# Loading the first query heads' output weights on five DMA engines instead of six, with half a head as half rows on all partitions

## Chip, cores, metric

One Trainium2 chip, one core. The metric is the device time of one execution in microseconds; lower is better. Verdicts use a 2% threshold, and the chip's "fast" state.

## The reference

One decode step: adaLN modulation, grouped-query attention over a cache, a small FFN. Cut to what matters:

```python
# x [1,1,512]; k_cache, v_cache [1,8,32768,128] bf16 (64 MB each); wq [512,4096]; wo [4096,512]
mod = (silu(c) @ w_mod).reshape(...)                   # six rows of 512
h = layernorm(x) * (1 + ca) + sa
q = h @ wq                                             # 32 query heads, 4 to each of 8 kv heads
o = softmax(q k^T / sqrt(128)) v
x = x + ga * (o @ wo)                                  # wo: 128 rows of 512 for each head
h = layernorm(x) * (1 + cb) + sb
x = x + gb * (relu(h @ w1) @ w2)
```

About 149 MB are read once for very little arithmetic, so the kernel is a stream of loads with a tail.

## The kernel before

The parts that matter: `wo` is loaded in five pieces. Piece 0, the first three heads, is called the low part below (`wo_lo` in the code). It lies on 48 of 64 partitions and comes in eight transfers of six partitions, 8 KB each, between the K and V tiles of two groups. Piece 1 is one head as one row on each of 128 partitions, and so on.

```python
WOP = [(0, 3, 48), (3, 1, P), (4, 4, P), (8, 16, P), (24, 8, P)]   # first head, heads, partitions
LO = [(0, 0, 16, 0), (1, 0, 8, 16), (1, 8, 16, 32), (2, 0, 16, 40)]
...
if kind == "wo_lo":
    b, i = key[1] // 4, key[1] % 4
    stream_dma(wo_lo[32 * b + i:32 * b + i + 21:4], wo_v(0)[24 * b + i:24 * b + i + 21:4])
...
elif kind == "wo_mid":                                  # pieces 1, 2, 3 in one buffer of the ring
    t = ring.tile([P, sum(wo_rows(i) for i in key[1:]), D], BF16, tag="slot", name="wo_sb")
    for i in key[1:]: ... stream_dma(loaded[("wo", i)], wo_v(i))
...
stream += [("v", LAST, (0, 1)), ("wo_mid", 1, 2, 3), ("v", LAST, (2,)), ("v", LAST, (3,)), ("wo", 4)]
stream += [("w1",)] + [("w2", i) for i in range(len(W2P))]
```

All loads are issued by SP into one queue, q1 of the profile. The profile has two more queues of the kind "instruction", q8 with packets of 16 KB and q14 with packets of 8 KB; they are called fetches below. The attention output is spread to the layout of each piece by masks (DVE) and one small matmul (`normalise`, `spread`), and multiplied with it (`project`).

## Time and profile before

| | kernel before |
|---|---|
| three first runs | 358.30, 357.19, 358.43 us |
| span of the traced run | 356.4 us |
| 16 DMA engines busy with the stream (q1) | 97.7% of the span |
| last packet of the stream | 352.20 us |
| from that packet to the end | 4.2 us |

The first thing to read is the share of q1 and the row of DMA digits, the second which DMA engine ends last. The profile has no view of single DMA engines. But the trace has start, duration and size of each packet, and an engine works without a pause, so a packet that starts where another one ended belongs to the same engine. This gives sixteen chains. Where two chains are in step to a few nanoseconds they can be mistaken for each other; the chains named below are kept apart by the packets that only they have. The prediction shows the lines; one more, on the transfers of piece 0, from the list of DMA issues (KB each):

```profile
wo_lo<-in_A_wo_dram SPq DMA_DIRECT2D x8, 48.0 KB
```

Eight issues of 48 KB, that is, 8 KB to each of six engines.

### The profile page before, as it was taken

The numbers are of one execution on the slowest core, as the hardware profiler recorded it, in microseconds if no ns is written. First come the engines' busy times: TensorE is split into PE (matmuls) and PEld (weight loads), VectorE is DVE, ScalarE is ACT, GpSimd is POOL, SyncE is SP. The second block draws the span as 40 slices with busy tenths as digits, with TensorE's granted clock in tenths as the row PEclk, the third lists the DMA queues.
The fourth block names the chain that finished last, engine by engine and source line by source line (L and its number), as shares of the span: only waits on it lengthen the run. The fifth ranks groups of instructions, "written<-read, shape, count | busy, mean of one in ns | idle before, by whom it ended". The sixth has DMA issues, their size and how long they took to land.

```text
span 356.4 us, 3625 instructions
## 1 busy us (share of the span) xinstructions
PE 287.4 (81%) x1554; PEld 127.7 (36%) x1554; DVE 194.1 (54%) x231; ACT 34.0 (10%) x78; POOL 12.0 (3%) x16
## 2 busy tenths in 40 slices
PE   0096766999779987999796969897987969899964
PEld 0053222334434443334242333333333323334563
DVE  5822967983397439372918256564718383742011
ACT  1012201301200120002000120012000100001200
POOL 9400000000000000000000000000000000000000
PEclk9999689899969998999896998999799979999855
DMA  8999999999999999999999999999999999999992
GB/s 326 436 427 443 423 449 424 423 451 425 423 436 434 421 451 434 425 436 423 440 434 423 452 426 416 452 428 414 449 430 427 440 427 445 434 411 419 428 414 83
DMA packets 6842, 149.66 MB, mean 420 GB/s; under 512 B 761, under 2 KB 890, under 8 KB 1914
## 3 DMA queue, kind: packets, MB, share of 16 engines
q1 hardware_dynamic: 6818, 149.43, 97.7%
q8 instruction: 12, 0.20, 0.2%
q14 instruction: 4, 0.03, 0.0%
q10 hardware_dynamic: 8, 0.00, 0.0%
HBM read 149.42 MB, written 0.00 MB: 419 GB/s over the span
## 4 chain that ended last, share of the span: by engine, by line
DMA 49%; PE 25%; DVE 19%; issue 5%; ACT 1%; POOL 0%; DVEq 0%; POOLq 0%
DMA Ksb<-in_A_k_cache_dram 42%; DVE KTt L413 14%; PE S_ps L422 11%; PE o_ps L496 8%; DMA Vsb<-in_A_v_cache_dram 5%; DMA w_sb<-in_B_w_dram 2%; DVE sel L184 2%; PE modT_ps L315 1%; PE mod_ps L298 1%; PE q_ps L298 1%; PE qT_ps L372 1%; PE acc_ps L486 1%; ACT L274 0%; DVE PT_g L465 0%; PE acc_ps L506 0%
## 5 line engine op out<-in xcount | busy, mean ns | idle before, releaser
L422 PE MATMUL S_ps<-KTt,qbd 128*128 128x512 bf16 x512 | 136.6, 425 | 34.4 <-DVE KTt L413 34.4
L413 DVE STREAM_TRANSPOSE KTt<-Ksb 128x2048 f32<-128x2048 f32 x64 | 142.6, 2280 | 29.3 <-DMA Ksb<-in_A_k_cache_dram 26.2
L496 PE MATMUL o_ps<-Vsb,PT_g 128*16 128x512 bf16 x480 | 108.4, 379 | 0.0
L422 PEld LDWEIGHTS <-qbd 128*128 128x128 bf16 x512 | 53.5, 105 | 111.2 <-issue 61.0
L496 PEld LDWEIGHTS <-PT_g 128*16 128x16 bf16 x480 | 40.8, 90 | 60.0 <-issue 5.9
L428 DVE TENSOR_SCALAR_CACHE_REDUCE S_g<-S_ps 128x512 f32<-128x512 f32 x16 | 11.1, 691 | 39.4 <-PE S_ps L422 39.4
L393 ACT COPY qbd<-qrep_sb 32x128 bf16<-32x128 bf16 x32 | 9.4, 295 | 160.6 <-PE S_ps L422 159.5
L465 DVE STREAM_TRANSPOSE PT_g<-P_g 128x1024 bf16<-128x1024 bf16 x8 | 9.9, 1238 | 21.7 <-ACT P_g L460 21.7
L514 DVE TENSOR_TENSOR oT_sb<-acc_ps,Linv 128x4 bf16<-128x4 f32 x8 | 1.3, 161 | 25.7 <-PE acc_ps L486 17.2
L234 PE MATMUL xc_ps<-one,c_bd 8*128 8x1 bf16 x4 | 0.3, 172 | 16.0 <-DVE rowsum L218 16.0
L506 PE MATMUL acc_ps<-osel,X 16*128 16x4 f32 x64 | 8.4, 250 | 2.5 <-ACT X L504 2.5
L457 ACT ACTIVATE nbias<-Mb_ps 128x1 f32<-128x1 f32 x8 | 1.4, 172 | 88.1 <-PE Mb_ps L455 88.1
L184 DVE COPY sel<-ident_bf 128x128 bf16<-128x128 bf16 x4 | 7.9, 3870 | 2.8 <-POOL ident_bf masks.py:199 2.8
L460 ACT ACTIVATE P_g<-S_g,nbias 128x1024 bf16<-128x1024 f32 x8 | 9.2, 1148 | 0.4 <-ACT nbias L457 0.2
L506 PEld LDWEIGHTS acc_ps<-osel,X 16*128 16x128 f32 x64 | 7.7, 186 | 3.7 <-ACT X L504 3.7
L444 DVE TENSOR_REDUCE Mrow<-mT_ps 1x4 f32<-1x128 f32 x8 | 2.2, 279 | 8.7 <-PE mT_ps L442 8.7
L504 ACT COPY X<-o_ps 16x512 f32<-16x512 f32 x8 | 4.6, 575 | 22.7 <-PE o_ps L496 22.7
L234 PEld LDWEIGHTS <-c_bd 8*128 8x128 bf16 x4 | 0.2, 114 | 16.0 <-DVE c_bd L224 16.0
L298 PE MATMUL q_ps<-wq_sb,hT 128*1 128x512 bf16 x32 | 3.6, 627 | 2.5 <-DVE hT L281 2.5
L473 DVE RECIPROCAL Linv<-L_ps 128x4 f32<-128x4 f32 x8 | 1.4, 176 | 7.0 <-PE L_ps L471 7.0
L486 PE MATMUL acc_ps<-PT_g,Vsb 128*128 128x4 bf16 x128 | 3.7, 166 | 1.6 <-DMA Vsb<-in_A_v_cache_dram 1.6
L455 PEld LDWEIGHTS Mb_ps<-ident_f,Mexp 1*128 1x128 f32 x16 | 2.3, 182 | 6.1 <-issue 6.1
(118 smaller groups left out, 102.3 us busy)
## 6 DMA issues: line engine op xcount, KB each, us to landing
Ksb<-in_A_k_cache_dram SPq DMA_DIRECT2D x16, 4096.0 KB, 29.1
Vsb<-in_A_v_cache_dram SPq DMA_DIRECT2D x15, 4096.0 KB, 23.5
wq_sb<-in_A_wq_dram SPq DMA_DIRECT2D x1, 4096.0 KB
Vsb<-in_A_v_cache_dram SPq DMA_DIRECT2D x2, 2048.0 KB, 22.7
wm_sb<-in_w_mod_dram SPq DMA_DIRECT2D x1, 3072.0 KB, 10.7
wo_sb<-in_A_wo_dram SPq DMA_DIRECT2D x1, 2048.0 KB
w_sb<-in_B_w_dram SPq DMA_DIRECT2D x1, 1792.0 KB
wo_sb<-in_A_wo_dram SPq DMA_DIRECT2D x1, 1024.0 KB, 11.1
```

The costliest lines, as they stand in the source:

```text
L184: nc.vector.tensor_copy(out=sel[:, hp, :].rearrange("p (a c) -> p a c", a=4), in_=src)
L298: nc.tensor.matmul(dst[j // 4][32 * (j % 4):32 * (j % 4) + 1, :], lhsT=src_T[:, kt:kt + 1], rhs=w[:, kt, j * 512:(j + 1) * 512], start=(kt ...
L393: nc.scalar.copy(out=o, in_=i)
L413: nc.vector.transpose(out=KTt[:].bitcast(F32), in_=Ksb[:, 32 * half:32 * half + 32, :].rearrange("p j d -> p (j d)").bitcast(F32),)
L422: nc.tensor.matmul(S_ps, lhsT=qbd[g % 2][:, hp, s, :], rhs=KTv[:, 16 * sl:16 * sl + 16, h, :, par], start=(t4 == 0 and sl == 0 and hp == 0 ...
L428: nc.vector.tensor_scalar(out=S_tiles[g][:, G, :], in0=S_ps, scalar1=1.0, scalar2=None, op0=ALU.mult, op1=ALU.max, accum_out=m_tiles[g][:, ...
L460: nc.scalar.activation(out=P_g[:], in_=S_g[:].rearrange("p g f -> p (g f)"), func=ACT.Exp, bias=nbias[:], scale=scale, accum_out=l_g[:],)
L465: nc.vector.transpose(out=PT_g[:], in_=P_g[:])
L486: nc.tensor.matmul(oT_ps, lhsT=Vsb[:, j, :], rhs=PT_g[:, j % 16, c0:c0 + REP], start=False, stop=(u == NTILE - 1 and j == TK - 1), skip_gr ...
L496: m = nc.tensor.matmul(o_tiles[g][:], lhsT=PT_g[:, j, REP * s0:REP * (s0 + 4)], rhs=Vsb.rearrange("p (s j) d -> p s j d", j=16)[:, :, j, : ...
L504: nc.scalar.copy(out=X[:], in_=o_tiles.pop(g)[:])
L506: nc.tensor.matmul(oT_ps, lhsT=X[:, s * Dh:(s + 1) * Dh], rhs=osel[:, s, :], start=(s == 0), stop=(g < LAST and s == 3), skip_group_check= ...
```

## The change

Its intent is to take the low part off one DMA engine: five partitions a transfer instead of six, and the 64 KB this leaves over (half of head 2) as 512 B half rows on all partitions, in the middle piece. `WOP` now counts rows: first row, rows on each partition, partitions. (The diff is shortened; `...` marks cuts.)

```diff
-    WOP = [(0, 3, 48), (3, 1, P), (4, 4, P), (8, 16, P), (24, 8, P)]
-    LO = [(0, 0, 16, 0), (1, 0, 8, 16), (1, 8, 16, 32), (2, 0, 16, 40)]
+    WOP = [(0, 8, 40), (320, 0.5, P), (3 * P, 1, P), (4 * P, 4, P), (8 * P, 16, P), (24 * P, 8, P)]
+    LO = [(0, 0, 16, 0), (1, 0, 4, 16), (1, 4, 16, 32), (2, 0, 8, 44)]
     def wo_v(i):
+        if i == 1:
+            return rows.rearrange("r (c d) -> (r c) d", c=2)
-            stream_dma(wo_lo[32 * b + i:32 * b + i + 21:4], wo_v(0)[24 * b + i:24 * b + i + 21:4])
+            stream_dma(wo_lo[32 * b + i:32 * b + i + 17:4], wo_v(0)[20 * b + i:20 * b + i + 17:4])
-    ... ("wo_mid", 1, 2, 3) ... ("wo", 4)
+    ... ("wo_mid", 1, 2, 3, 4) ... ("wo", 5)
-    for n in sorted({wo_rows(i) for i in range(len(WOP))}):
+    for n in (1, 2, 4, 8, 16):                              # one mask pair more
     # normalise, group 0: one large mask more; spread(1) multiplies by the row's parity
+            nc.vector.tensor_tensor(out=oA[1][:], in0=oT_sb[:, 2:3]..., in1=cmask[1][:, 64:P]..., op=ALU.mult)
+            nc.vector.tensor_tensor(out=o2[:], in0=o2_ps[:].to_broadcast([P, 2]), in1=parity[:], op=ALU.mult)
     # project(1): two matmuls of 256 columns, one for each half of a row
+                for c in range(2):
+                    nc.tensor.matmul(a_rows[0][32 * c:32 * c + 1, c * D // 2:(c + 1) * D // 2], ...)
```

More of the change, by code (lines that the diff above doesn't have):

```diff
@@ L1 @@
 from contextlib import ExitStack
+import math
 import concourse.bass as bass
@@ L68, in wo_v @@
     def wo_v(i):
-        h0, n, pp = WOP[i]
-        return A_wo[h0 * Dh:(h0 + n) * Dh, :].rearrange("(p r) d -> p r d", p=pp)
-    def wo_rows(i):
-        return WOP[i][1] * Dh // WOP[i][2]
+        r0, n, pp = WOP[i]
+        rows = A_wo[r0:r0 + int(n * pp), :]
+        if i == 1:
+            return rows.rearrange("r (c d) -> (r c) d", c=2)
+        return rows.rearrange("(p r) d -> p r d", p=pp)
     w1_v = B_w1.rearrange("(p kt) f -> p kt f", p=P)
@@ L116, in load @@
         elif kind == "wo":
-            t = ring.tile([P, wo_rows(key[1]), D], BF16, tag="slot", name="wo_sb")
+            t = ring.tile([P, WOP[key[1]][1], D], BF16, tag="slot", name="wo_sb")
             src = wo_v(key[1])
         elif kind == "wo_mid":
-            t = ring.tile([P, sum(wo_rows(i) for i in key[1:]), D], BF16, tag="slot", name="wo_sb")
+            t = ring.tile([P, sum(math.ceil(WOP[i][1]) for i in key[1:]), D], BF16, tag="slot", name="wo_sb")
             r0 = 0
             for i in key[1:]:
-                loaded[("wo", i)] = t[:, r0:r0 + wo_rows(i), :]
-                r0 += wo_rows(i)
+                n = math.ceil(WOP[i][1])
+                loaded[("wo", i)] = t[:, r0, 0:D // 2] if i == 1 else t[:, r0:r0 + n, :]
+                r0 += n
                 stream_dma(loaded[("wo", i)], wo_v(i))
@@ L151 @@
                     stream.append(("wo_lo", 4 * (g - 1) + 2 * G + (kind == "v")))
-    stream += [("v", LAST, (0, 1)), ("wo_mid", 1, 2, 3), ("v", LAST, (2,)), ("v", LAST, (3,)), ("wo", 4)]
+    stream += [("v", LAST, (0, 1)), ("wo_mid", 1, 2, 3, 4), ("v", LAST, (2,)), ("v", LAST, (3,)), ("wo", 5)]
     stream += [("w1",)] + [("w2", i) for i in range(len(W2P))]
@@ L163 @@
     wm_sb = need(("wm",))
-    wo_lo = const.tile([64, wo_rows(0), D], BF16)
+    wo_lo = const.tile([64, 8, D], BF16)
     nc.gpsimd.memset(wo_lo[:], 0.0)
@@ L205 @@
         nc.vector.tensor_copy(out=rsel[n][:], in_=rsel_f[:])
+        if n == 2:
+            parity = rsel_f
     osel = const.tile([16, 4, REP], F32)
@@ L209 @@
     oT_sb = const.tile([P, Hq], BF16)
-    oA = [const.tile([P, n, P // wo_rows(i)], BF16, name=f"oA{i}") for i, (_, n, _) in enumerate(WOP)]
-    oA[0] = const.tile([P, 1, 64], BF16, name="oA_lo")
+    oA = [const.tile([P, 64], BF16, name="oA0"), const.tile([P, 64, 2], BF16, name="oA1")]
+    oA += [const.tile([P, n, P // n], BF16, name=f"oA{i}") for i, (_, n, _) in enumerate(WOP) if i > 1]
     nc.gpsimd.memset(oA[0][:], 0.0)
@@ L514, in normalise @@
         nc.vector.tensor_tensor(out=o_g, in0=oT_ps, in1=Linv_tiles.pop(g)[:], op=ALU.mult)
-        for i, (h0, n, _) in enumerate(WOP):
+        if g == 0:
+            for h, ca, cb, p0 in LO:
+                nc.vector.tensor_tensor(
+                    out=oA[0][:, p0:p0 + cb - ca], in0=oT_sb[:, h:h + 1].to_broadcast([P, cb - ca]),
+                    in1=cmask[8][:, ca:cb], op=ALU.mult,
+                )
+            nc.vector.tensor_tensor(
+                out=oA[1][:], in0=oT_sb[:, 2:3].unsqueeze(2).to_broadcast([P, 64, 2]),
+                in1=cmask[1][:, 64:P].unsqueeze(2).to_broadcast([P, 64, 2]), op=ALU.mult,
+            )
+            spread(0)
+            spread(1)
+        for i in range(2, len(WOP)):
+            r0, n, _ = WOP[i]
+            h0 = r0 // Dh
             ha, hb = max(h0, REP * g), min(h0 + n, REP * (g + 1))
@@ L518, in normalise @@
                 continue
-            RH = wo_rows(i)
-            if i == 0:
-                for h, ca, cb, p0 in LO:
-                    nc.vector.tensor_tensor(
-                        out=oA[0][:, 0, p0:p0 + cb - ca], in0=oT_sb[:, h:h + 1].to_broadcast([P, cb - ca]),
-                        in1=cmask[RH][:, ca:cb], op=ALU.mult,
-                    )
-            else:
-                shape = [P, hb - ha, Dh // RH]
-                nc.vector.tensor_tensor(
-                    out=oA[i][:, ha - h0:hb - h0, :], in0=oT_sb[:, ha:hb].unsqueeze(2).to_broadcast(shape),
-                    in1=cmask[RH][:].unsqueeze(1).to_broadcast(shape), op=ALU.mult,
-                )
+            shape = [P, hb - ha, Dh // n]
+            nc.vector.tensor_tensor(
+                out=oA[i][:, ha - h0:hb - h0, :], in0=oT_sb[:, ha:hb].unsqueeze(2).to_broadcast(shape),
+                in1=cmask[n][:].unsqueeze(1).to_broadcast(shape), op=ALU.mult,
+            )
             if hb == h0 + n:
@@ L537, in spread @@
     def spread(i):
-        pp, RH = WOP[i][2] if i else 64, wo_rows(i)
-        o2_ps = small_ps([pp, RH], "o2_ps")
-        nc.tensor.matmul(
-            o2_ps[:], lhsT=oA[i][:].rearrange("p h c -> p (h c)"), rhs=rsel[RH][:], start=True, stop=True,
-        )
-        o2 = const.tile([pp, RH], BF16, name=f"o2_sb{i}")
-        nc.vector.tensor_copy(out=o2[:], in_=o2_ps[:])
+        pp, n = (64, 8) if i == 0 else (P, math.ceil(WOP[i][1]))
+        o2_ps = small_ps([pp, n], "o2_ps")
+        lhsT = oA[i][:] if i == 0 else oA[i][:].rearrange("p a b -> p (a b)")
+        nc.tensor.matmul(o2_ps[:], lhsT=lhsT, rhs=rsel[n][:], start=True, stop=True)
+        if i == 1:
+            o2 = const.tile([P, 2], BF16, name="o2_sb1")
+            nc.vector.tensor_tensor(out=o2[:], in0=o2_ps[:].to_broadcast([P, 2]), in1=parity[:], op=ALU.mult)
+        else:
+            o2 = const.tile([pp, n], BF16, name=f"o2_sb{i}")
+            nc.vector.tensor_copy(out=o2[:], in_=o2_ps[:])
         o2_tiles[i] = o2
     def project(i):
-        n = wo_rows(i)
+        n = WOP[i][1]
         wo_sb = need(("wo", i))
@@ L554, in project @@
                 a_rows.append(row_bank("a_ps"))
+            if i == 1:
+                for c in range(2):
+                    nc.tensor.matmul(
+                        a_rows[0][32 * c:32 * c + 1, c * D // 2:(c + 1) * D // 2], lhsT=o2_tiles[1][:, c:c + 1],
+                        rhs=wo_sb, start=False, stop=False, skip_group_check=True,
+                    )
+                return
             for r in range(n):
```

## The prediction

> **What bounds the kernel now.** I read the page first: the row of slices, the queues and the chain that ended last.
>
> ```profile
> span 356.4 us, 3625 instructions
> ...
> DMA  8999999999999999999999999999999999999992
> ...
> q1 hardware_dynamic: 6818, 149.43, 97.7%
> q8 instruction: 12, 0.20, 0.2%
> q14 instruction: 4, 0.03, 0.0%
> ```
>
> From the second slice to the 39th the sixteen DMA engines are busy 90% or more, and queue q1 alone fills 97.7% of their time: the kernel is a stream of 149 MB. The next question is whether some stage of the stream waits for buffers. I set the issue times of the loads against the start of their first packets in the trace. A 4 MB load moves in about 9.7 us, and from the start to the last V tiles each load is issued 6.6 to 26 us before its first packet; the shortest leads are 6.65 us (the first K half of group 2) and 7.25 us (the last V step). After that the lead shrinks to 3.4 us (last piece of wo), 3.1 (w1), 2.95, 2.06 and 1.18 (the three pieces of w2), but the queue still isn't empty. So PE, DVE and SP are beside the stream until its last load lands, and only the stream's length and the tail behind it set the end. The chain of waits, in order of time, has that tail:
>
> ```profile
> 323.98 17.39 DMA Vsb<-in_A_v_cache_dram
> ...
> 341.41 1.88 PE acc_ps L486 x64
> 343.30 0.02 issue
> 343.31 8.59 DMA w_sb<-in_B_w_dram
> 351.90 0.04 issue
> 351.94 0.60 PE ffn_ps L645 x16
> 352.54 0.04 issue
> 352.58 0.41 PE ffn_ps L645 x8
> 352.99 0.02 issue
> 353.01 0.30 DVE o_rows L651
> ```
>
> The last matmuls start at 352.58 because the last piece of w2 has just landed. What follows (8 matmuls, two DVE operations, the store) takes 356.4 - 352.2 = 4.2 us and isn't touched.
>
> A load has landed when its slowest DMA engine is through. The trace has start, duration and size of every packet, and an engine's packets lie back to back, so they can be linked into sixteen chains. All 4,096 packets of 32 KB have a median of 1,213 ns: no engine is slower per packet. But the chains don't end together. The six that carry the eight 8 KB packets of the low part of wo end their last w2 packet at 352.20, 351.21, 350.57, 349.95, 349.6 and 349.5 us; of the ten others one ends at 350.27 and the rest between 347.5 and 349.4. One engine is 1 us behind the next and about 3.5 us behind the middle of the field. It began its stream early; what put it back is the eight 8 KB packets, 312 ns each from period to period (9,993 ns from one to the next, against 9,681 for a plain 4 MB load), hence 2.50 us, and two instruction fetches of queue q8, at 33 and 314 us. Each took a gap of 0.87 us plus a packet of 1,764 instead of 1,213 ns: 1.42 us. The second-last engine has the same wo load and two fetches of 8 KB (q14), 0.83 and 0.84 us.
>
> **What the Trainium skill says.** "DMA: Bandwidth & Descriptors", section "Why a DMA increments its semaphore by 16 and not by 1": a transfer issued by SP runs on the largest number k of engines, at most 16, that divides the slowest dimension of both sides, and on the lowest-numbered k. Six partitions then mean engines 0 to 5, five mean 0 to 4. The trace agrees for six: the 48 packets of 8 KB fall in eight groups of six, always on the same six chains. Five no run here shows yet. "Runtime: NRT & Kernel Launch", section "Instruction fetch mechanics": instructions come in blocks of 16 KiB, over a DMA queue of the sequencer's own. The trace agrees: the twelve packets of q8 have 16,384 B. The DMA page's "Bandwidth" section, on small descriptors, gives a fixed overhead per packet, so half rows of 512 B should cost little more than their bytes; I size them from the trace below.
>
> **The change part by part.**
>
> *Low part of wo.* Eight transfers of 6 x 8 KB become eight of 5 x 8 KB. Engines 0 to 4 keep 8 x 312 ns = 2.50 us each; engine 5 loses all of it.
>
> *Half rows.* The 64 KB set free come as 128 runs of 512 B, eight an engine. A packet of 1 KB took 46 ns and one of 2 KB 84, which is 37 ns per KB over some 8 ns fixed: 27 ns for 512 B (an estimate). Starts of consecutive 1 KB packets lie 42 ns apart, four less than their duration, so 8 x 23 plus some 9 for the semaphore packet = 0.19 us on every engine.
>
> *Sum per engine.* Engine 5: -2.50 + 0.19 = -2.31 us. All others: +0.19 us. Bytes are the same.
>
> *Issue.* The eight small issues stay (0.70 us each on SP); one of about 0.35 us is added ahead of the middle piece of wo. It goes out at 306.7 for packets that start at 319.9, 13 us of lead: hidden.
>
> *Front.* A row count of 2 is new, so DVE builds one more mask pair: 0.19 + 0.28 + 0.07 = about 0.54 us on the front's DVE chain at 13 to 15 us. The loads that wait for the front have 16 to 17 us of lead, those of the following groups at least 6.6: hidden.
>
> *Normalise of group 0.* At 96.5 us DVE makes four small masks, one large (0.28 us) and two casts. One LO row shortens, one large multiply (0.3 us) is added, a 128x2 multiply takes the place of one cast (the head's own spread keeps another), and PE gets one more 0.2 us spread. Together at most 0.7 us, at a place where the stream's lead is over 9 us: hidden.
>
> *Projection.* Two matmuls of 256 columns join 21 of 512 that take about 1.8 us at 332 to 335 us. At most 0.2 us later, w1's buffer comes free; w1 had 3.1 us of lead, and PE later stands idle 1.7 us for the last V step. Hidden.
>
> So all that counts is which engine ends last. If engine 5 is the one that now ends at 352.20, it falls to about 349.9, and the next, 351.21 + 0.19 = 351.40, becomes the last: -0.80 us at the end of the stream. The landing of the last V step is set by the same two chains (341.0 and 340.0 us), so attention's tail moves by the same amount and doesn't eat it. If engine 5 is one of the other five, the last engine only gets the half rows: +0.19 us.
>
> **Rivals.**
>
> 1. *Engine 5 isn't the last.* The trace numbers no engine. For it being the last: fetches of q8 go round eight engines (the ninth hits the same as the first), of which this one alone is among the six, one is 6 or 7, and six carry neither c's eight small packets nor wo's, so they are 8 to 15; a fetching set that reaches high is likelier to include 5 than 0 to 4. Engine 0 can be excluded, since its chain has the single 1 KB packet of x. Against it: that is all. And a change so fiddly is made by someone who has seen that sixth engine lag. I give it 75%. Otherwise +0.2 us.
>
> 2. *A fetch takes the place of the saving.* The fetches fall where the instruction count puts them; a dozen more instructions could move one of 1.4 us onto another loaded engine, or into the last 20 us. The second-last engine would then be the last at about 352.4. The order round the engines speaks against it. It would make the change worth nothing to +0.5 us.
>
> 3. *A wait replaces a transfer.* The extra transfer shifts the completion semaphores by one, so a late load could wait for an earlier one. The lead of the w2 pieces is 1.2 to 3 us, and loads eight before them have landed by then. Worth at most a few tenths; unlikely.
>
> 4. *The average counts, not the last engine* (bytes are the same, so nothing changes, 0.0). Against it: the tail's wait ends within 0.4 us of the slowest chain's last packet.
>
> **Range and chances.** The stated 358.3 is the median of 357.19, 358.30 and 358.43; such a median may come out some tenths lower when repeated, so I take 358.2. With 75% at -0.80, 25% at about +0.2: 358.2 - 0.6 + 0.05 = 357.6 us. The runs before spread by 1.2 us, more than the effect, so the range is 356.7 to 358.6. Two per cent would be 7.2 us; nothing that the change touches is that large (the whole low part of wo costs 2.5 us on an engine). Within 2%: 97%; faster 2%, slower 1%.
>
> **What would show it.** In the changed kernel's trace: 40 packets of 8 KB from the low part, on five chains; 128 packets of 512 B near 320 us, about 27 ns each; the chain with two fetches of q8 without 8 KB packets of wo's low part and ending near 350 us; the last packet of w2 near 351.4 instead of 352.2, on the chain with the two 8 KB fetches; DMA digits unchanged; front and normalise later by half a microsecond without idle time in the stream. The prediction is wrong if the twice-fetching chain still has the 8 KB packets (then +0.2), if gaps other than fetches appear in the chains, or if the tail behind the last packet is longer than 4.2 us.

## The result, and the profile after

357.42 us, median of 357.28, 357.36, 357.48 and 357.55, against 357.78 for the kernel before, median of 357.19, 357.26, 358.30 and 358.43. Ratio 0.9989, 95% interval 0.9966 to 1.0012: the same at 2%, and the interval includes 1. A later series gave 0.9986 (0.9966 to 1.0006).

The page of the changed kernel, same lines as before:

```profile
span 355.4 us, 3638 instructions
...
DMA  8999999999999999999999999999999999999993
...
q1 hardware_dynamic: 6946, 149.43, 98.0%
q8 instruction: 12, 0.20, 0.2%
q14 instruction: 4, 0.03, 0.0%
```

Still a full stream with the same bytes, 1.0 us shorter; q1 has 128 packets more, the half rows. Its DMA issues of `wo`'s early pieces (KB each; the 17.4 is us from issue to landing):

```profile
wo_lo<-in_A_wo_dram SPq DMA_DIRECT2D x8, 40.0 KB
wo_sb<-in_A_wo_dram SPq DMA_DIRECT2D x1, 128.0 KB, 17.4
wo_sb<-in_A_wo_dram SPq DMA_DIRECT2D x1, 64.0 KB
```

The chain of waits at the end (start us, length us, what):

```profile
323.91 16.54 DMA Vsb<-in_A_v_cache_dram
340.45 0.05 issue
340.50 1.88 PE acc_ps L491 x64
342.38 0.02 issue
342.39 8.62 DMA w_sb<-in_B_w_dram
...
351.69 0.41 PE ffn_ps L667 x8
352.10 0.02 issue
352.12 0.30 DVE o_rows L673
```

The last V tile is used at 340.50 instead of 341.41, the last eight matmuls start at 351.69 instead of 352.58, and everything behind keeps its length. In the packets: 40 of 8 KB in the low part's time on five chains, 128 of 512 B at 27 ns, and the last packet of w2 at 351.34 instead of 352.20. It is now on the chain that had two 8 KB fetches. The chain that is gone from the low part is the one with the two 16 KB fetches (at 33.0 and 314.0 us), so that chain is engine 5. (No trace numbers the engines; here and below the numbers follow from the rule that the prediction cites.)

The added work beside the stream, DVE in the normalisation of group 0 (start us, busy us, engine, line, operation, operands, count), before and then after:

```profile
96.22 0.16 DVE L514 TENSOR_TENSOR oT_sb<-acc_ps,Linv 128x4 bf16<-128x4 f32 x1 [1.22 <-PE acc_ps L506]
...
97.19 0.35 DVE L545 CAST o_sb<-o_ps 64x8 bf16<-64x8 f32 x2
97.45 2.30 DVE L413 STREAM_TRANSPOSE KTt<-Ksb 128x2048 f32<-128x2048 f32 x1
```

```profile
96.51 0.16 DVE L519 TENSOR_TENSOR oT_sb<-acc_ps,Linv 128x4 bf16<-128x4 f32 x1 [1.22 <-PE acc_ps L511]
...
97.30 0.28 DVE L539 TENSOR_TENSOR oA<-oT_sb,cmask 128x128 bf16<-128x128 bf16 x1
97.51 0.15 DVE L560 CAST o_sb<-o_ps 64x8 bf16<-64x8 f32 x1
97.66 0.16 DVE L557 TENSOR_TENSOR o_sb<-o_ps,rsel_f 128x2 bf16<-128x2 f32 x1
97.91 0.16 DVE L560 CAST o_sb<-o_ps 128x1 bf16<-128x1 f32 x1
97.99 2.30 DVE L418 STREAM_TRANSPOSE KTt<-Ksb 128x2048 f32<-128x2048 f32 x1
```

From the first operation to the next transpose it takes 1.48 instead of 1.23 us, and it starts 0.3 us later. None of it reaches the end, where the same tail comes 0.9 us earlier.

So the pair of traces shows what was predicted, and a bit more of it: -0.86 us at the last packet. But the four runs of each kernel don't. The changed kernel's lie within 0.3 us; those of before are two near 357.2 and two near 358.4, and the traced one (358.14) is of the slower kind. A steady saving of 0.8 would have made the four into two groups near 356.4 and 357.6. This was the open question for the experiments.

### The profile page after: what moved, and what is told of

Read it like the earlier page. It is cut to its first block, busy times and chain, and to the rows that moved or that the text cites. A ratio compares the mean times of both kernels' runs of the same rounds, so it can differ in the third digit from the quotient of the medians. Undisturbed runs are those within 1.5% of the kernel's fastest.

```text
span 355.4 us, 3638 instructions
## 1 busy us (share of the span) xinstructions
PE 287.3 (81%) x1557; PEld 128.0 (36%) x1557; DVE 194.9 (55%) x236; ACT 34.0 (10%) x78; POOL 12.0 (3%) x16
## 4 chain that ended last, share of the span: by engine, by line
DMA 49%; PE 25%; DVE 19%; issue 5%; ACT 1%; POOL 0%; DVEq 0%; POOLq 0%
DMA Ksb<-in_A_k_cache_dram 42%; DVE KTt L418 14%; PE S_ps L427 11%; PE o_ps L501 8%; DMA Vsb<-in_A_v_cache_dram 5%; DMA w_sb<-in_B_w_dram 2%; DVE sel L186 2%; PE modT_ps L320 1%; PE mod_ps L303 1%; PE q_ps L303 1%; PE qT_ps L377 1%; PE acc_ps L491 1%; ACT L279 0%; DVE rsel_f L203 0%; DVE PT_g L470 0%
## 5 line engine op out<-in xcount | busy, mean ns | idle before, releaser
L303 PE MATMUL mod_ps<-wm_sb,siluT 128*1 128x512 bf16 x24 | 3.6, 624 | 1.1 <-DVE siluT L297 1.1
```

Source lines behind the costliest of these rows:

```text
L303: nc.tensor.matmul(dst[j // 4][32 * (j % 4):32 * (j % 4) + 1, :], lhsT=src_T[:, kt:kt + 1], rhs=w[:, kt, j * 512:(j + 1) * 512], start=(kt ...
```

## The experiments

Theory: the end is set by the DMA engine that ends last, whatever the mean does. Rivals: the mean load counts; the added or removed work of PE and DVE counts; and, for the two groups, something in the start or the tail differs instead of the stream.

**The kernel before against itself** (no edit).

> The kernel before, unchanged, against itself. Its four runs so far lie in two groups, 357.2 and 358.4 us. Theory (the engine that ends last): the groups differ in what delays the last engine; in a trace of a 358.4 run (span about 356.4) the last packet of w2 comes at 352.2 on the chain with two 16 KB fetches and the low wo packets; in a trace of a 357.2 run (span about 355.3) that chain ends about 1 us earlier and the one with two 8 KB fetches (351.2) is the last. Rival (the tail or the start differs, not the stream): a 357.2 run has the same last packet near 352.2 and a shorter tail than 4.2 us. Ratio 1.000, within 0.002.

Measured: 357.13 to 358.61 us (median 358.38, ratio 1.001). Of the 11 reference runs in this series five lie between 357.10 and 357.42 and six between 358.32 and 358.56; nothing between. The traced run took 358.61, with the last packet at 352.57:

```profile
342.51 9.77 DMA w_sb<-in_B_w_dram
352.28 0.04 issue
352.32 0.60 PE ffn_ps L645 x16
```

Here the 16 KB fetches hit engine 5 not at 33 and 314 us but at 109 and 345. The delay shows in the low packets: the chain that starts a low packet at 107.49 starts the next at 118.91, 1.42 us later than the 9.99 of the other groups. Hence the new theory on the groups. The fetches visit eight engines in a fixed order, but the place at which the round begins differs from run to run. The packets that they stretch show it: in the first trace these take 1,764, 1,762, 1,707, 1,712, 1,719, 1,681, 1,672 and 1,694 ns, and here the same row comes, to some 10 ns, two places earlier (1,681, 1,694, 1,764, 1,764, 1,707, ...). Twelve fetches over eight engines means two for four of them. Engine 5 gets two or one, and one fetch is 1.42 us.

**Five engines, the half head left out** (half a head is missing. Its output is wrong, which doesn't matter for the time. The comparison still called it correct, so it doesn't notice half a head).

```diff
-                stream_dma(loaded[("wo", i)], wo_v(i))
+                if i != 1:
+                    stream_dma(loaded[("wo", i)], wo_v(i))
...
             if i == 1:
+                return
                 for c in range(2):
```

> The changed kernel without the half rows (transfer and two matmuls taken out; wrong result on purpose). Theory: all chains end 0.19 us earlier than in the changed kernel, the last packet of w2 near 351.15 instead of 351.34, time about 357.2. Rival (the mean load of the engines sets the end): 64 KB less is 0.04% of the bytes, 0.15 us less; cannot be told from the theory here, but the half rows' price is read from it. Rival (the added DVE and PE work costs): nothing changes, since spread and masks are kept.

Measured: 357.20 us (357.09 to 357.54), last packet 351.28, against 351.34 for the changed kernel (0.06 earlier, expected 0.19) and 357.42. The chains of one engine begin up to half a microsecond apart from run to run, so single traces can't size 0.19. The transfer itself can be read in the changed kernel: its eight packets begin at 321.388 and the first 1 KB packet behind them at 321.582, 0.194 us.

**Six engines, and the half rows besides.**

```diff
-            t = ring.tile([P, sum(wo_rows(i) for i in key[1:]), D], BF16, tag="slot", name="wo_sb")
-            r0 = 0
+            t = ring.tile([P, 1 + sum(wo_rows(i) for i in key[1:]), D], BF16, tag="slot", name="wo_sb")
+            r0 = 1
+            stream_dma(t[:, 0, 0:D // 2], A_wo[0:64, :].rearrange("r (c d) -> (r c) d", c=2))
```

> The kernel before, and the half rows loaded besides (64 KB more, not used). Theory: every chain +0.19 us, so the last packet at the kernel before's plus 0.19, and none of the saving: slower than the changed kernel by 0.2 to 1.2 us, according to which group of the kernel before it falls into. Rival (the gain came from the half rows' smaller transfers or from the fourth piece of the middle load): as fast as the changed kernel.

Measured: 357.16, 357.25, 357.43, 357.47 and 358.50, 358.58: both groups, as the kernel before, so the half rows didn't bring the gain. The traced run, 357.47, is of the fast group, and it is the trace that tells most about it. Its end (chain of waits):

```profile
351.81 0.04 issue
351.85 0.41 PE ffn_ps L646 x7
352.26 0.02 issue
```

Engine 5 is hit by a 16 KB fetch once in it, at 242 us, and ends at 351.26, though it has all its low packets and the half rows; the chain with two 8 KB fetches ends at 351.50 and is last. In the two slow traces so far engine 5 was hit twice.

**Four engines**: heads 0 and 1 in the low part, heads 2 and 3 as two rows on all partitions.

```diff
-    WOP = [(0, 3, 48), (3, 1, P), (4, 4, P), (8, 16, P), (24, 8, P)]
-    LO = [(0, 0, 16, 0), (1, 0, 8, 16), (1, 8, 16, 32), (2, 0, 16, 40)]
+    WOP = [(0, 2, 32), (2, 2, P), (4, 4, P), (8, 16, P), (24, 8, P)]
+    LO = [(0, 0, 16, 0), (1, 0, 16, 32)]
-            stream_dma(wo_lo[32 * b + i:32 * b + i + 21:4], wo_v(0)[24 * b + i:24 * b + i + 21:4])
+            stream_dma(wo_lo[32 * b + i:32 * b + i + 13:4], wo_v(0)[16 * b + i:16 * b + i + 13:4])
```

> Two heads on four engines (8 transfers of 4 x 8 KB), heads 2 and 3 as two rows on all partitions: engine 4 gives up its low packets too, all engines get 0.3 us more than in the kernel before (eight 2 KB packets for eight 1 KB ones). Theory with the twice-8-KB-fetched chain being engine 4: that chain ends near 349.0 and the next, about 350.4 to 350.6, becomes last: 0.7 us faster than the changed kernel, about 356.7. If it is one of engines 0 to 3: last packet near 351.45, 357.5, no gain. The 16 KB fetches say engine 5; the order says nothing of engine 4: even chances. Rival (mean load sets the end): same as the changed kernel.

Measured: 357.40 us (357.32 to 357.61), last packet 351.41, on the chain with two 8 KB fetches, which still has low packets. So that engine isn't 4, and taking the load off another one of the six brought nothing. The mean rival says the same here; the next two runs part them.

**Two more looks at the kernel before.**

> The kernel before again, one look. New theory, of the two groups of its times: the 16 KB fetches go round eight engines, always in the same order, but start at another place in each execution; there are twelve of them, so four engines get two and four get one. If engine 5 gets two (two of the four places of the start seen so far), it ends last, near 352.2 to 352.6, and the run takes 358.2 to 358.6 us. If it gets one, the chain with two 8 KB fetches is last, near 351.2, and the run takes 357.1 to 357.5. Either way time and number of fetches on engine 5 go together. Rival (the start of the stream varies): they don't.

> As before_look_2: one more look at the kernel before, to have a trace of its other group. Two fetches on engine 5: 358.2 to 358.6 us and the last packet near 352.4; one: 357.1 to 357.5 and near 351.2.

Measured: 358.35 and 358.34 us, last packets 352.42 and 352.41, engine 5 hit twice in both (the first, at 33 us, shows in the low packets: its first one comes at 88.77, those of four other chains at 87.1 to 87.5). All nine reference runs of this series, on another chip than the last, were of the slow group too: 358.22 to 358.63.

**Three engines**, after the pattern of the change.

```diff
-    WOP = [(0, 8, 40), (320, 0.5, P), (3 * P, 1, P), (4 * P, 4, P), ...]
-    LO = [(0, 0, 16, 0), (1, 0, 4, 16), (1, 4, 16, 32), (2, 0, 8, 44)]
+    WOP = [(0, 8, 24), (192, 0.5, P), (2 * P, 2, P), (4 * P, 4, P), ...]
+    LO = [(0, 0, 12, 0), (0, 12, 16, 32), (1, 0, 8, 36)]
-            stream_dma(wo_lo[32 * b + i:32 * b + i + 17:4], wo_v(0)[20 * b + i:20 * b + i + 17:4])
+            stream_dma(wo_lo[32 * b + i:32 * b + i + 9:4], wo_v(0)[12 * b + i:12 * b + i + 9:4])
-                out=oA[1][:], in0=oT_sb[:, 2:3]...
+                out=oA[1][:], in0=oT_sb[:, 1:2]...
```

> One and a half heads on three engines (8 transfers of 3 x 8 KB), the other half head as half rows, heads 2 and 3 as two rows on all partitions. In the run with four engines the twice-8-KB-fetched chain kept its low packets and ended last at 351.41, so it is one of engines 0 to 3. Theory, if it is engine 3: it loses 2.5 us, and the last is one with two 16 KB fetches at 350.3 to 350.6 plus 0.5, about 350.9: 0.4 to 0.5 us faster than the changed kernel. If it is 0 to 2: last packet near 351.6, 0.2 us slower than the changed kernel. Rival (mean load): same as the changed kernel.

Measured: 356.64 us (356.42 to 356.99), ratio to the kernel before 0.9951 (0.9938 to 0.9963), last packet 351.04. The low packets are now on three chains, none of which had an 8 KB fetch before them, so the chain with two 8 KB fetches is engine 3. The last chain is now one with two 16 KB fetches, as expected, at 77 and 336 us. The traced run, 356.99, is the slowest of the five. The end of its chain of waits:

```profile
342.21 8.52 DMA w_sb<-in_B_w_dram
350.73 0.04 issue
350.77 1.00 PE ffn_ps L667 x22
```

**Two engines**: one head in the low part, heads 1 to 3 in pieces of one and two rows on all partitions.

```diff
-    WOP = [(0, 3, 48), (3, 1, P), (4, 4, P), ...]
-    LO = [(0, 0, 16, 0), (1, 0, 8, 16), (1, 8, 16, 32), (2, 0, 16, 40)]
+    WOP = [(0, 1, 16), (1, 1, P), (2, 2, P), (4, 4, P), ...]
+    LO = [(0, 0, 8, 0), (0, 8, 16, 32)]
-            stream_dma(wo_lo[32 * b + i:32 * b + i + 21:4], wo_v(0)[24 * b + i:24 * b + i + 21:4])
+            stream_dma(wo_lo[32 * b + i:32 * b + i + 5:4], wo_v(0)[8 * b + i:8 * b + i + 5:4])
-    ... ("wo_mid", 1, 2, 3) ... ("wo", 4)
+    ... ("wo_mid", 1, 2, 3, 4) ... ("wo", 5)
```

> One head on two engines (8 transfers of 2 x 8 KB), heads 1 to 3 in pieces of one and two rows on all partitions (0.64 us more on every engine than in the kernel before). Theory, if the twice-8-KB-fetched chain is engine 2 or 3: it ends near 349.4, the last is a chain with two 16 KB fetches at about 350.9 to 351.2: 0.2 to 0.4 us faster than the changed kernel. If it is 0 or 1: last packet near 351.85, 0.4 us slower than the changed kernel. Rival (mean load): same as the changed kernel.

Measured: 356.64 us (356.54 to 356.74), ratio 0.9951 (0.9937 to 0.9965), last packet 350.77. The engine hit by fetches at 32.8 and 312.6 us, engine 5 by its place in the round, is in this trace too; without low packets it ends at 350.53, not last. The chain with two 8 KB fetches, engine 3, ends at 349.33 (expected 349.4), and the last has two 16 KB fetches at 77 and 336 us. The end of the chain of waits:

```profile
344.16 6.95 DMA w_sb<-in_B_w_dram
351.11 0.04 issue
351.15 0.41 PE ffn_ps L645 x8
```

The mean load is the same in all these kernels but for packet overhead, which *grows* from six engines to two. The time falls all the same: the mean doesn't set the end.

**The changed kernel again, and looks at the kernel before.**

> The changed kernel again. Theory (the start of the fetches' round differs from run to run, and engine 5 no longer can be last): one group of times, 357.2 to 357.6, wherever the round starts; the last packet near 351.3 to 351.4 on engine 3, the chain with two 8 KB fetches. Ratio to the kernel before 0.997 if all of its runs are of the slow group (358.2 to 358.6), 1.000 if all are of the other (357.1 to 357.5). Rival (the change shortened something else by a fixed amount): the ratio is the same whatever group the kernel before is in.

> The kernel before, one look, hoped to fall into the fast group. As before_look_2: with one 16 KB fetch on engine 5, 357.1 to 357.5 us and the last packet near 351.2 to 351.5 on engine 3; with two, 358.2 to 358.6 and near 352.4 on engine 5.

> One more look at the kernel before, for the same reason. With one 16 KB fetch on engine 5, 357.1 to 357.5 us and the last packet near 351.2 to 351.5 on engine 3; with two, 358.2 to 358.6 and near 352.4 on engine 5.

> The kernel before a last time, for a trace of its fast group; the run with six engines and half rows (357.47 us, one 16 KB fetch on engine 5, last packet 351.50) stands in for it so far. With one 16 KB fetch on engine 5: 357.0 to 357.5 us and the last packet near 351.2 to 351.5, on engine 3; with two: 358.1 to 358.6 and near 352.1 to 352.6, on engine 5. The theory falls if a run of about 357.2 shows two fetches on engine 5, or one of about 358.4 only one.

Measured: the changed kernel 357.11 to 357.23 us in six runs, one group, last packet 351.30. In the same series the kernel before had six runs of 358.06 to 358.44 (mean 358.28) and five of 356.84 to 357.12 (mean 356.98). Against the mean of the changed kernel, 357.17, that is -1.11 us and +0.19 us (in the first series, split in the same way, -0.95 and +0.19). Looks 4 and 5 took 358.22 and 358.06 us, last packets 352.30 and 352.13; look 6 was traced at 358.40, 352.47, and one of its other runs took 357.09. All three have two fetches on engine 5. So of seven traces of the kernel before, seven are slow and have two; a fast one was never caught in a trace. For the fast group stand only the six-engine run with half rows, the +0.19 us, and a sum: in the seven slow traces the chain with two 8 KB fetches is second-last and ends 0.98 to 1.25 us before engine 5. With one fetch (1.42 us) less on engine 5 that chain would be last, and the run that much shorter, which is an estimate from these traces; the two groups lie 1.14 to 1.30 us apart in the four series that have both.

| traced run | 16 KB fetches on engine 5 | low packets on it | last packet, us | time, us |
|---|---|---|---|---|
| before, seven traces | 2 | 8 | 352.13 to 352.57 | 358.06 to 358.61 |
| six engines and half rows | 1 | 8 | 351.50 (another engine) | 357.47 |
| changed, first trace | 2 | 0 | 351.34 (another engine) | 357.28 |
| two engines | 2 | 0 | 350.77 (another engine) | 356.64 |

Three and two engines are the versions with the earliest ends: on their chip 1.77 and 1.76 us below the mean of the kernel before (358.39), whose runs there were all of the slow group, against 1.11 for the changed kernel on its chip. That comparison goes over two chips, with the slow group as the common measure; the two were never timed beside the changed kernel, so that they beat it by 0.65 is likely but not shown. It is also more than the 0.2 to 0.5 us that were expected; the last packets, 351.04 and 350.77 against 351.30, differ by 0.26 and 0.53.

## Why the prediction was right or wrong

- **The stream's last engine sets the end: right.** The last packet and the end moved together (-0.86 and -1.0 us in the first pair of traces), and kernels with the same bytes differ by where the bytes go. (One reading was off, though nothing rests on it: by the prediction's own list of ends the last engine is about 3 us behind the middle of the field, not 3.5.)
- **-2.50 us for engine 5, +0.19 for all: right.** The low packets left exactly one chain, the other five keep 9.993 us from one low packet to the next. 512 B took the estimated 27 ns, all eight 0.194 us.
- **Engine 5 is the last: right** in the slow group, from which the trace came; given at 75%.
- **Engine 5 falls to about 349.9:** it ended at 350.25, and its chain was already 0.34 us later at the first fetch than in the trace before, which is the whole difference. It isn't last, so this didn't matter.
- **Hidden parts: right.** The front's DVE chain came 0.47 us later (the SiLU result starts at 17.75 instead of 17.28), the shortest lead of a load early on fell from 6.65 to 6.34 us, and no chain paused. Group 0's normalisation took 0.25 us more; the two half-row matmuls ran between others and the issues of w1 and w2 began at 335.37 instead of 335.44.
- **"-0.80 us at the end of the stream" for every run: wrong for about half of them.** I took one trace for all. It was of the slow group, in which engine 5 is hit twice; the prediction's own list of three times had 357.19 beside 358.30 and 358.43, and I took that as spread. In the slow group the saving was 1.11 (0.95 in the first series), in the fast one there was none and the half rows' 0.19 remained. Half of each gives 0.46, and measured was 0.39 (0.0011 of 358).
- **Rival 2** (a fetch takes the place of the saving) came near the cause with the wrong mechanism. It let added instructions move a fetch onto another loaded engine of the changed kernel; but the runs of one kernel differ, so the round begins elsewhere by itself, and what it takes away is the lag of engine 5 in the kernel before. In the changed kernel's ten runs (357.11 to 357.55 us) no such loss showed.

The number, 357.6 for a measured 357.42, came out well for a reason that isn't quite its own: the saving was weighted with the 75% for engine 5, and what really takes a part of it away is the half of the runs in which engine 5 isn't last. What decides where the round begins stays open: one of the five series had only slow reference runs, the other four had both kinds.

## What to carry to other kernels

When a stream is bound by DMA, look at the engine that ends last, not at the mean busy share; the 64 KB that the change moved between engines were worth 0.3% against the slow group and nothing against the fast one, and the 192 and 256 KB of the versions with three and two engines 0.5% against the slow group, with not one byte less. Before a trace is taken as *the* behaviour, compare its time with all runs: two groups of times want two traces. And a load that is put on few engines is best kept off those that a trace shows to be held up by instruction fetches as well.

## What the Trainium skill lacked or had wrong

- "Runtime: NRT & Kernel Launch", "Instruction fetch mechanics", calls the cost of crossing a 16 KiB boundary "mostly hidden" and doesn't say what the fetch costs the data that share its DMA engine. In a stream that fills all DMA engines it isn't hidden: each 16 KB fetch among the 32 KB packets put one engine back 1.42 us (on engine 5 a gap of 0.87 and a packet of 1,764 instead of 1,213 ns).
- The same section gives blocks of 16 KiB only. The packets of q14, which the profile calls instruction too, have 8,192 B; two of them cost their engine 0.83 and 0.84 us. Whether they are fetches of the kind that the section means, no run shows.
- No page says which DMA engines the fetches use, or that it changes from run to run: here the 16 KB ones go round eight engines, engine 5 among them, twelve to an execution, from different places in different runs.
- "DMA: Bandwidth & Descriptors", "Why a DMA increments its semaphore by 16 and not by 1", names its choice of engines as seen for 16, 10, 2 and 1 of them. The number held here for six, five, four, three and two partitions (as many chains with low packets); that they are the lowest-numbered engines no trace here shows.
